# float64 weights to float32 words: the sign's word made on GpSimd, the magnitude scaled on ScalarE

## The chip, the cores and the metric

The kernel runs on one core of one Trainium2 chip. The metric is the device time of one execution in microseconds (us); the time given for a kernel is the median of its runs. PE is TensorE, DVE is VectorE, ACT is ScalarE, POOL is GpSimd, and SP is SyncE, whose queue issues most of the transfers.

## The reference, cut to what matters

Three blocks are computed in a row: windowed attention with a linear bias (4 batches, 8 heads, 576 positions, 64 columns a head), a gated MLP with a mixing over positions (width 512, inner width 1024), and a second MLP with a convolution of three taps and a sigmoid gate.

```python
x = attention(q, k, v)                       # (4, 576, 512)
h = gelu(x @ w_in);  u, v = h[..., :512], h[..., 512:]
v_s = einsum('ts,bsd->btd', w_sg, layernorm(v) * g_ln) + b_sg
x = x + (u * v_s) @ w_out
h = relu(x @ w_in2)
out = (h * sigmoid(conv3(h))) @ w_out2
```

`w_in`, `w_out`, the convolution's taps and the second MLP's two weights are drawn as float64 and are handed to the kernel as they are. [...]

## The kernel before, in words

Every large product is made in float32 accuracy out of three products of rounded operands: a matrix is split into a rounded part `hi` and a remainder `lo` (`split`, L244), and PE adds hi*hi, hi*lo and lo*hi. A weight therefore goes through a load, the conversion of its float64 words to float32 (`narrowed`, L310), a rounding (on ACT as a rule) and a remainder (on POOL as a rule) before PE can use it.

`narrowed` takes a staged block of n numbers in each of 128 partitions, as 2n 32-bit words: `low` is every first word, `high` every second one, which holds the sign, 11 bits of exponent and 20 bits of mantissa. It reads the high word as if it were a float32. The steps are: the magnitude of the high word into the tile `wa` (an Abs on ACT at L322 if `act_abs` is set, else a bit mask on DVE at L324); a clamp of it between W_LOW and W_HIGH on DVE (L328), which bounds the exponent; a mask and a shift left by three bits (L329); the sign bits of the high word are or-ed in (L330); and the low word's upper three bits, shifted down by 29, are or-ed in (L331). The last two have two tensor inputs. So DVE does four steps for a block whose magnitude comes from ACT, and five for the others.

`w_in` comes in eight pieces of 512 columns (`w_in_load` L345, `w_in_piece` L350, steps `j` and `i` of the order), the second half first; ACT makes the magnitude for the four pieces of the second half and for the first one of the first half. Four staging buffers are used in turn, so the load of the fifth piece waits until the first has been converted. `w_out` comes in eight pieces of 256 columns (`w_out_piece` L373, step `o`), all with the magnitude on DVE; their `wa` tiles have two buffers in turn. The second MLP's weights go through the same function later (`w2_piece` L382), as do the taps (L894).

The order of the work is a list of steps written by hand (L54 to L130). A framework then orders each engine's instructions out of it by priority and by a simulated timeline, except where an instruction is kept behind the one written before it on its engine (`keep_in_program_order`). Up to about 80 us the four batches' first attention heads, the pieces of w_in and the first products run interleaved; from there on the first batch's mixing (`m_sg` L827, step `G`), the weights' scaling (`a_norm` L495, step `N`, through `scaled` L233), the transposes of the attention weights (`a_transpose` L532, step `T`) and the product with w_out (`m_wo` L848, step `W`).

Where several engines could do a step, a planner picks one while the program is written out. It keeps a ledger of nanoseconds for each engine, which never falls more than SLACK (6000 ns) behind PE's:

```python
def book(eng, ns):
    load[eng] = max(load[eng], load["pe"] - SLACK) + ns
def pick(costs):
    eng = min(costs, key=lambda e: max(load[e], load["pe"] - SLACK) + costs[e])
    book(eng, costs[eng])
```

The costs are formulas of the columns n. `narrowed` books 67 + 0.52 n on DVE for the clamp (L327) and 200 + 2.6 n for the other steps (L332). Of the steps that the planner can place, those of interest here are the scaling of attention weights (DVE or POOL), the gate's rounding (ACT, DVE or POOL) and its remainder (DVE or POOL), and the copies of transposed weights out of PSUM (ACT or DVE).

Of the kernel before, what the change touches and what calls it, by code (L numbers as in the profile page):

```python
# [11 lines left out]
AF = mybir.ActivationFunctionType  # L12
ALU = mybir.AluOpType
# [5 lines left out]
HF = FF // 2  # L19
# [16 lines left out]
NVN = 4  # L36
# [12 lines left out]

W_LOW = 2.0**-15  # L50
W_HIGH = 122879.9921875


def _steps():  # L54
# [80 lines left out]
def attention_gmlp_glu_kernel(  # L135
# [21 lines left out]
    nc = tc.nc  # L157
    PSUM = bass.MemoryType.PSUM

    def f(ap):  # L160
        return ap.bitcast(F32)
# [39 lines left out]
# [6 lines that stand above are left out]
        return eng  # L207
# [36 lines left out]
    def split(hi, lo, src, kind=None, done=None):  # L244

        ins = copy(hi, src, kind is None, ON[kind + " hi"] if kind else "act dve")
        if done is not None:
            done[:] = [ins.ins.name]
        return tt(lo, src, f(hi), ALU.subtract, ON[kind + " lo"] if kind else "dve")
# [7 lines left out]
    mpool = p1.enter_context(tc.tile_pool(name="mpool", bufs=2))  # L257

    with tc.using_default_side("right"):
        pa = ExitStack()  # L260
        apool = pa.enter_context(tc.tile_pool(name="apool", bufs=2))
# [27 lines left out]
    for i in range(NP):  # L289
        st = cpool.tile([P, 18], F32, name=f"st{i}")  # L290
# [16 lines left out]

    STAGE = dict(st=S, vn=1024, w64=512)

    def narrowed(src, n, pool, tag, bufs, spool, stag, sbufs, act_abs=False):  # L310

        if spool is None:
            st = src
        else:
            st = spool.tile([P, STAGE[stag]], U32, tag=stag, name="w64", bufs=sbufs)
            dma = nc.sync.dma_start(st[:, : 2 * n], src)
            later(dma)
        words = st[:, : 2 * n].rearrange("p (n w) -> p n w", w=2)
        low, high = words[:, :, 0], words[:, :, 1]
        a = pool.tile([P, 256 if tag == "wa" else 512], U32, tag=tag, name="wa", bufs=bufs)[:, :n]  # L320
        if act_abs:
            tc.keep_in_program_order(nc.scalar.activation(f(a), f(high), AF.Abs))  # L322
        else:
            ins = tc.keep_in_program_order(nc.vector.tensor_scalar(a, high, 0x7FFFFFFF, None, op0=ALU.bitwise_and))  # L324
            if last_hi:
                tc.add_manual_dep(ins.ins, last_hi[-1], follow, reason="high part first")
        clamp = nc.gpsimd if pick({e: c for e, c in dict(dve=67 + 0.52 * n, pool=147 + 0.93 * n).items() if e in ON["clamp"]}) == "pool" else nc.vector  # L327
        tc.keep_in_program_order(clamp.tensor_scalar(f(a), f(a), W_LOW, W_HIGH, op0=ALU.max, op1=ALU.min))  # L328
        nc.vector.tensor_scalar(a, a, 0x07FFFFFF, 3, op0=ALU.bitwise_and, op1=ALU.logical_shift_left)  # L329
        nc.vector.scalar_tensor_tensor(a, high, 0xC0000000, a, op0=ALU.bitwise_and, op1=ALU.bitwise_or)  # L330
        nc.vector.scalar_tensor_tensor(a, low, 29, a, op0=ALU.logical_shift_right, op1=ALU.bitwise_or)  # L331
        book("dve", 200 + 2.6 * n)  # L332
        return f(a)

    def cols(w, k, c0, n):

        return w.bitcast(U32)[:, k, 2 * c0 : 2 * (c0 + n)]

    w64, last_in, last_win, last_hi = {}, [], [], []

    def later(dma):

        tc.add_manual_dep(dma.ins, last_in[0].ins.name, follow, reason="later")
# [4 lines left out]
        last_in[:] = [tc.keep_in_program_order(nc.sync.dma_start(st, w_in.bitcast(U32)[:, half, k, :]))]  # L348

    def w_in_piece(half, k):  # L350
        a = narrowed(w64.pop((half, k)), HF, mpool, "u", 4, None, "vn", NVN, half == 1 or k == 0)
        if half:
            split(winh[:, k, HF:], winl[:, k, HF:], a, "win")
        else:
            sl = slice(k * P, (k + 1) * P)
            last_win[:] = [split(winh[:, :, sl], winl[:, :, sl], a.rearrange("p (k n) -> p k n", k=NK), "win" if k else "win u", None if k else last_hi)]

    def staged(src, dtype):
        st = mpool.tile([P, S], dtype, tag="x", name="wst", bufs=8)[:, : src.shape[-1]]
        later(nc.sync.dma_start(st, src))  # L360
        return st
# [11 lines left out]
    def w_out_piece(k, half):  # L373
        if k == half == 0:
            kept["wo"] = w1pool.tile([P, NK, 2, 2, 256], F32R, tag="wo", name="wo")
        st = staged(cols(w_out, k, half * 256, 256), U32)
        a = narrowed(st, 256, apool, "wa", 2, None, "x", 8)
        split(kept["wo"][:, k, half, 0, :], kept["wo"][:, k, half, 1, :], a, "wo")

    p2pool = []  # L380
# [491 lines left out]
    def constants(i):  # L872
# [11 lines left out]
        B=rotations,  # L884
        k=constants, l=z_load, v=z_vload, c=z_scores, e=z_exp, n=z_norm, t=z_transpose, z=z_av, j=w_in_load, L=a_load, M=a_vload, C=a_scores, E=a_exp, N=a_norm, T=a_transpose, A=a_av,
        X=a_xsplit, V=m_v, U=m_u, G=m_sg, W=m_wo, i=w_in_piece, g=w_sg_piece, o=w_out_piece, a=w2_piece,
    )

# [230 lines left out]
```

## Time and profile before

| what | value |
|---|---|
| median of 3 runs | 543.5 us (542.86 to 543.69) |
| the profiled execution's own time | 543.29 us |
| its span, from the first to the last instruction | 541.1 us |
| mean granted clock of TensorE | 0.997 of full speed |
| busy share PE, DVE, ACT, POOL | 96%, 68%, 48%, 45% |
| instructions | 11980 |

Shares of the span are averages over stretches with different limits. A group of instructions is read as: line, engine, operation, output<-input by the program's names, shapes and count, then busy time, the mean length of one, and the idle time before them with what ended it.

### The profile page before, as it was taken

To read this page: it belongs to the slowest core of one execution; us is meant where nothing else is said; L and a number is where in the kernel's file an instruction comes from. 1 tells how busy PE (TensorE), PEld (TensorE's weight loads), DVE (VectorE), ACT (ScalarE), POOL (GpSimd) and SP (SyncE) were. 2 spreads that over 40 slices of the span, in tenths; PEclk is the share of its full clock that TensorE was granted. 3 is DMA by queue.
4 is the path that set the end of the run, shared out by engine and by line. 5 is a ranking of instruction groups with operands and counts; after the bars stand their busy time and mean duration, and the time that the engine had idled before them with its cause. 6 is when DMAs were issued, how large, how long until landed. Compare 5 with 4: busy or idle time off the path is not lost.

```text
span 541.1 us, 11980 instructions
## 1 busy us (share of the span) xinstructions
PE 520.7 (96%) x4548; PEld 474.7 (88%) x4548; DVE 367.7 (68%) x959; ACT 258.7 (48%) x673; POOL 243.2 (45%) x383
## 2 busy tenths in 40 slices
PE   8997989999998999999999999999999999999997
PEld 6776879898898988989988999998998999999887
DVE  4999798754878875879767688687567354654300
ACT  6694578342458451376534434452554333444310
POOL 2444238542146363246453344245586545465500
PEclk9999989999999999999999999999999999999999
DMA  8974541433261765243643433902202100100011
GB/s 290 394 241 175 150 121 52 148 113 98 89 201 37 218 187 190 82 124 92 173 144 115 155 101 131 337 13 52 75 21 81 66 22 19 42 21 27 33 39 59
DMA packets 33209, 63.93 MB, mean 118 GB/s; under 512 B 3968, under 2 KB 13952, under 8 KB 33152
## 3 DMA queue, kind: packets, MB, share of 16 engines
q1 hardware_dynamic: 33008, 63.04, 35.8%
q8 instruction: 36, 0.59, 0.5%
q14 instruction: 21, 0.17, 0.1%
q10 hardware_dynamic: 144, 0.13, 0.1%
HBM read 48.47 MB, written 14.68 MB: 117 GB/s over the span
## 4 chain that ended last, share of the span: by engine, by line
PE 62%; DVE 14%; ACT 9%; POOL 7%; DMA 5%; issue 3%; SPq 0%; ACTq 0%; DVEq 0%; POOLq 0%
PE psg L213 31%; PE psv L213 7%; PE pso L213 6%; PE psu L213 5%; PE o L213 4%; ACT t L186 3%; PE pss L213 3%; PE sc L213 3%; POOL t L242 3%; PE pT L515 2%; DMA w<-in_w_in_dram 2%; DVE t L451 1%; DVE wa L330 1%; DMA kq<-in_qk_dram 1%; DVE wa L328 1%
## 5 line engine op out<-in xcount | busy, mean ns | idle before, releaser
L213 PEld LDWEIGHTS psg<-x2g,w 128*128 128x128 f32 x768 | 103.1, 188 | 2.4 <-ACT hb L973 0.7
L213 PE MATMUL psg<-x2g,w 128*128 128x256 f32 (+1 forms) x768 | 104.6, 294 | 0.6 <-ACT hb L973 0.5
L213 PE MATMUL psg<-wout,gh 128*128 128x512 f32 (+1 forms) x272 | 80.1, 378 | 0.0
L186 ACT ACTIVATE t<-t,st 128x192 f32<-128x192 f32 (+1 forms) x144 | 61.9, 431 | 15.0 <-DVE st L451 15.0
L213 PE MATMUL pss<-wsg,vn 128*128 128x256 f32 (+1 forms) x448 | 63.6, 298 | 3.6 <-DVE t L843 3.0
L213 PEld LDWEIGHTS pss<-wsg,vn 128*128 128x128 f32 x448 | 60.5, 190 | 4.7 <-DVE t L843 4.0
L977 DVE SCALAR_TENSOR_TENSOR cc<-hb,cw,cc 128x576 f32<-128x576 f32 x32 | 26.6, 832 | 46.9 <-POOL cc L242 46.9
L213 PEld LDWEIGHTS psg<-wout,gh 128*128 128x128 f32 x272 | 49.8, 188 | 8.7
L213 PE MATMUL psu<-xg,win 128*128 128x320 f32 (+1 forms) x384 | 54.2, 298 | 2.6 <-ACT win L222 1.7
L213 PEld LDWEIGHTS psu<-xg,win 128*128 128x128 f32 x384 | 51.7, 188 | 3.7 <-ACT win L222 1.8
L213 PE MATMUL pso<-gh,wo 128*128 128x256 f32 (+1 forms) x256 | 51.8, 300 | 0.5 <-DVE t L843 0.5
L213 PE MATMUL psg<-wout,gl 128*128 128x512 f32 (+1 forms) x136 | 50.9, 378 | 0.0
L213 PE MATMUL psv<-win,xg 128*128 128x512 f32 x192 | 47.6, 398 | 0.9 <-DVE wa L328 0.9
L242 POOL TENSOR_SCALAR cc<-hb,cw 128x576 f32<-128x576 f32 x32 | 28.3, 885 | 42.7 <-ACT hb L973 42.7
L451 DVE CUSTOM_DVE_ANT_0 t<-sc,tab 128x192 f32<-128x192 f32 (+1 forms) x144 | 40.4, 335 | 5.4 <-PE sc L213 5.0
L973 ACT ACTIVATE hb<-psg 128x576 f32<-128x576 f32 x32 | 20.7, 651 | 47.5 <-PE psg L213 45.0
L213 PEld LDWEIGHTS psv<-win,xg 128*128 128x128 f32 x192 | 35.5, 188 | 8.7 <-ACT win L222 1.0
L231 DVE TENSOR_TENSOR gg<-cc,hb 128x576 f32<-128x576 f32 x32 | 30.1, 943 | 17.2 <-ACT cc L186 17.0
L213 PEld LDWEIGHTS pso<-gh,wo 128*128 128x128 f32 x256 | 40.3, 188 | 1.7 <-DVE t L843 1.2
L213 PE MATMUL pso<-gl,wo 128*128 128x256 f32 (+1 forms) x128 | 36.9, 301 | 1.3 <-POOL gl L231 0.6
L231 POOL TENSOR_TENSOR t<-t,u 128x256 f32<-128x256 f32 (+1 forms) x32 | 27.2, 854 | 18.6 <-DVE t L843 18.4
L231 POOL TENSOR_TENSOR gl<-gg,gh 128x512 fp32r<-128x512 f32 x24 | 33.7, 1404 | 0.6
(101 smaller groups left out, 960.4 us busy)
## 6 DMA issues: line engine op xcount, KB each, us to landing
V<-in_v_dram SPq DMA_DIRECT2D x12, 704.0 KB, 4.7
x2s<-x2d SPq DMA_DIRECT2D x16, 288.0 KB, 2.9
w<-in_w_in_dram SPq DMA_DIRECT2D x8, 512.0 KB, 7.5
w<-in_w_out_dram SPq DMA_DIRECT2D x16, 256.0 KB, 3.2
w<-in_w_in_dram SPq DMA_DIRECT2D x16, 256.0 KB, 2.8
wout<-w2d SPq DMA_DIRECT2D x8, 512.0 KB, 6.0
q<-in_q_dram SPq DMA_DIRECT2D x12, 320.0 KB, 4.0
out_dram<-ot SPq DMA_DIRECT2D x15, 256.0 KB, 2.0
```

What stands on the lines that cost most here:

```text
L186: ins = nc.scalar.activation(*args, **kw)
L213: return nc.tensor.matmul(out, lhsT, rhs, start=start, stop=stop, **kw)
L231: return (nc.vector if eng == "dve" else nc.gpsimd).tensor_tensor(dst, a, b, op=op)
L242: e.tensor_scalar(dst, src, col, 1.0, op0=ALU.mult, op1=ALU.mult)
L328: tc.keep_in_program_order(clamp.tensor_scalar(f(a), f(a), W_LOW, W_HIGH, op0=ALU.max, op1=ALU.min))
L330: nc.vector.scalar_tensor_tensor(a, high, 0xC0000000, a, op0=ALU.bitwise_and, op1=ALU.bitwise_or)
L451: nc.vector.tensor_tensor_reduce(e, bank, table, scale=-SCALE, scalar=3e38, op0=ALU.add, op1=ALU.min, accum_out=mx)
L515: ins = nc.tensor.transpose(ps[:, i * P : (i + 1) * P], src, ident)
L973: nc.scalar.activation(h[:, 1 : S + 1], ps[:, 256 : 256 + S], AF.Relu)
L977: nc.vector.scalar_tensor_tensor(cc, h[:, 0:S], cw[:, 0, c : c + 1], cc, op0=ALU.mult, op1=ALU.add)
```

## The change

For the pieces of w_in and w_out (`apart` = 1) the steps are replaced. ACT makes the magnitude and multiplies it by 2^-48 in the same step, for all sixteen pieces. POOL multiplies the high word, read as a float32, twice by 2^-140 and writes it back in place, strided: what is left is a zero with the word's sign. DVE clamps the magnitude between the bounds scaled by the same 2^-48. After that the exponent's field lies so that the shift by three needs no mask. DVE shifts the low word down by 29 and ors the signed zero in, in place in the staging buffer; then it shifts the magnitude left by three and ors that word in. DVE so does three steps for every piece. The planner is told 200 + 1.6 n on DVE in all, for the clamp and both other steps. The second MLP's weights and the taps stay as they were, and so do the loads and buffers.

```diff
@@ -49,6 +49,8 @@
 
 W_LOW = 2.0**-15
 W_HIGH = 122879.9921875
+W_DOWN = 2.0**-48
+W_GONE = 2.0**-140
 
 
 def _steps():
@@ -307,7 +309,7 @@
 
     STAGE = dict(st=S, vn=1024, w64=512)
 
-    def narrowed(src, n, pool, tag, bufs, spool, stag, sbufs, act_abs=False):
+    def narrowed(src, n, pool, tag, bufs, spool, stag, sbufs, act_abs=False, apart=0):
 
         if spool is None:
             st = src
@@ -318,6 +320,19 @@
         words = st[:, : 2 * n].rearrange("p (n w) -> p n w", w=2)
         low, high = words[:, :, 0], words[:, :, 1]
         a = pool.tile([P, 256 if tag == "wa" else 512], U32, tag=tag, name="wa", bufs=bufs)[:, :n]
+        if apart:
+            tc.keep_in_program_order(nc.scalar.activation(f(a), f(high), AF.Abs, scale=W_DOWN))
+            ins = tc.keep_in_program_order(
+                nc.gpsimd.tensor_scalar(f(high), f(high), W_GONE, W_GONE, op0=ALU.mult, op1=ALU.mult)
+            )
+            clamp = nc.gpsimd if apart == 2 else nc.vector
+            tc.keep_in_program_order(
+                clamp.tensor_scalar(f(a), f(a), W_LOW * W_DOWN, W_HIGH * W_DOWN, op0=ALU.max, op1=ALU.min)
+            )
+            nc.vector.scalar_tensor_tensor(low, low, 29, high, op0=ALU.logical_shift_right, op1=ALU.bitwise_or)
+            nc.vector.scalar_tensor_tensor(a, a, 3, low, op0=ALU.logical_shift_left, op1=ALU.bitwise_or)
+            book("dve", 200 + 1.6 * n)
+            return f(a)
         if act_abs:
             tc.keep_in_program_order(nc.scalar.activation(f(a), f(high), AF.Abs))
         else:
@@ -348,7 +363,7 @@
         last_in[:] = [tc.keep_in_program_order(nc.sync.dma_start(st, w_in.bitcast(U32)[:, half, k, :]))]
 
     def w_in_piece(half, k):
-        a = narrowed(w64.pop((half, k)), HF, mpool, "u", 4, None, "vn", NVN, half == 1 or k == 0)
+        a = narrowed(w64.pop((half, k)), HF, mpool, "u", 4, None, "vn", NVN, half == 1 or k == 0, 1)
         if half:
             split(winh[:, k, HF:], winl[:, k, HF:], a, "win")
         else:
@@ -374,7 +389,7 @@
         if k == half == 0:
             kept["wo"] = w1pool.tile([P, NK, 2, 2, 256], F32R, tag="wo", name="wo")
         st = staged(cols(w_out, k, half * 256, 256), U32)
-        a = narrowed(st, 256, apool, "wa", 2, None, "x", 8)
+        a = narrowed(st, 256, apool, "wa", 2, None, "x", 8, apart=1)
         split(kept["wo"][:, k, half, 0, :], kept["wo"][:, k, half, 1, :], a, "wo")
 
     p2pool = []
```

## Rows read from the trace of the kernel before

**Rows 1.** The page: busy us by engine (part 1), granted clock in forty slices (part 2).

```profile
PE 520.7 (96%) x4548; PEld 474.7 (88%) x4548; DVE 367.7 (68%) x959; ACT 258.7 (48%) x673; POOL 243.2 (45%) x383
...
PEclk9999989999999999999999999999999999999999
```

**Rows 2.** Stretches of the span: busy us and count (x) by engine, granted clock, DMA.

```profile
13.50:76.80 63.30, 55.92 (x663) 45.84 (x662) 57.25 (x166) 42.03 (x112) 25.68 (x33) 1.00 0.63 223
76.80:101.00 24.20, 22.85 (x210) 21.06 (x210) 22.11 (x74) 17.20 (x68) 19.74 (x35) 0.93 0.25 80
101.00:150.00 49.00, 49.00 (x537) 44.86 (x536) 31.51 (x111) 18.79 (x47) 15.03 (x33) 1.00 0.35 114
150.00:541.00 391.00, 381.76 (x2986) 353.68 (x2984) 250.46 (x570) 171.62 (x413) 179.17 (x272) 1.00 0.31 98
```

**Rows 3.** What PE waited for, 13.5 to 101 us: total, times, longest.

```profile
PE sc L213 <- DVE st L451: 2.1, 1, 2.1
PE psu L213 <- ACT win L222: 1.7, 1, 1.7
PE o L213 <- ACT ph L222: 1.2, 2, 1.0
PE psv L213 <- DVE wa L328: 0.9, 1, 0.9
```

**Rows 4.** Short stretches around PE's longest wait, columns as in rows 2.

```profile
76.00:78.00 2.00, 1.23 (x20) 1.26 (x22) 2.00 (x15) 2.00 (x10) 0.00 (x0) 0.68 0.78 296
78.00:80.00 2.00, 2.00 (x14) 1.88 (x10) 1.97 (x8) 2.00 (x10) 0.16 (x1) 0.50 0.05 9
80.00:82.00 2.00, 2.00 (x18) 2.00 (x18) 2.00 (x17) 2.00 (x11) 1.32 (x2) 0.97 0.82 230
```

**Rows 5.** VectorE's steps on wa, 13.5 to 76.8 us: ns least/median/most, first and last start.

```profile
L328 DVE TENSOR_SCALAR wa<-wa x11: 274/416/1385, 13.6 to 69.1; 128x512 f32<-128x512 f32 x8, 128x256 f32<-128x256 f32 x3
L329 DVE TENSOR_SCALAR wa<-wa x11: 267/427/1525, 14.0 to 69.7; 128x512 uint32<-128x512 uint32 x8, 128x256 uint32<-128x256 uint32 x3
L330 DVE SCALAR_TENSOR_TENSOR wa<-w,wa x8: 675/688/1655, 15.0 to 53.0; 128x512 uint32<-128x512 uint32 x8
...
L324 DVE TENSOR_SCALAR wa<-wst x4: 274/283/286, 59.0 to 74.0; 128x256 uint32<-128x256 uint32 x4
L324 DVE TENSOR_SCALAR wa<-w x3: 415/420/421, 37.1 to 50.1; 128x512 uint32<-128x512 uint32 x3
```

**Rows 6.** VectorE in order of time, near 22 us: start us, length us, instruction.

```profile
22.34 1.52 DVE L329 TENSOR_SCALAR wa<-wa 128x512 uint32<-128x512 uint32 x1
```

**Rows 7.** GpSimd in order of time, near 22 us, same columns.

```profile
22.32 1.27 POOL L231 TENSOR_TENSOR win<-wa,win 128x512 fp32r<-128x512 f32 x1 [0.88 <-ACT win L222]
```

**Rows 8.** GpSimd's groups by form, whole span: busy us, mean ns, idle before.

```profile
L242 POOL TENSOR_SCALAR t<-t,r 128x192 f32<-128x192 f32 x49 | 22.7, 476 | 0.0
...
L231 POOL TENSOR_TENSOR win<-wa,win 128x512 fp32r<-128x512 f32 x8 | 11.2, 1402 | 8.4 <-ACT win L222 7.1 <-DVE win L224 1.3
...
L225 POOL TENSOR_SCALAR wh<-wa 128x256 fp32r<-128x256 f32 x20 | 9.2, 461 | 41.6 <-DVE wa L331 41.4
...
L231 POOL TENSOR_TENSOR wo<-wa,wo 128x256 fp32r<-128x256 f32 x8 | 6.3, 793 | 11.3 <-ACT wo L222 11.3
...
L225 POOL TENSOR_SCALAR x2g<-x2s 128x576 fp32r<-128x576 f32 x4 | 3.1, 778 | 0.0
```

**Rows 9.** ScalarE's magnitude step L322.

```profile
L322 ACT ACTIVATE wa<-w x17: 424/438/686, 12.9 to 332.3; 128x256 f32<-128x256 f32 x12, 128x512 f32<-128x512 f32 x5
```

**Rows 10.** VectorE's steps on wa, 76.8 to 101 us.

```profile
L329 DVE TENSOR_SCALAR wa<-wa x5: 280/286/347, 77.8 to 95.2; 128x256 uint32<-128x256 uint32 x5
L330 DVE SCALAR_TENSOR_TENSOR wa<-wst,wa x5: 409/417/523, 78.2 to 95.5; 128x256 uint32<-128x256 uint32 x5
```

**Rows 11.** VectorE's groups by form, 76.8 to 101 us.

```profile
L242 DVE TENSOR_SCALAR t<-t,r 128x192 f32<-128x192 f32 x6 | 2.8, 513 | 0.0
...
L224 DVE COPY ph<-pT 128x512 f32<-128x512 f32 x3 | 2.0, 676 | 0.0
```

## The prediction, made before the changed kernel was run

> **What bounds the kernel now.** I read the page's totals first, then the stretches of the span, then what TensorE waited for, and only then single steps. The totals show TensorE (PE) busy for 520.7 of 541.1 us and VectorE (DVE) for 368 [rows 1]. Read alone, that says nothing done to DVE can matter. The stretches say where it can [rows 2]. From 13.5 to 76.8 us DVE is busy 57.25 of 63.3 us and PE only 55.92, so PE stands idle for 7.4 us in a stretch where DVE is nearly full. From 76.8 to 101 us DVE is busy 22.1 of 24.2 us, GpSimd (POOL) 19.7, and PE is idle for 1.4. From 101 to 150 us PE is busy throughout, and in the 391 us after that it idles for 9.2 us in all. So time can be won before 101 us, and PE's queue carries a head start won there to the end.
>
> Of PE's waits before 101 us, two end behind DVE [rows 3]: 2.1 us for the statistics of the masked scores (line 451), and 1.7 us for a piece of w_in, which ScalarE (ACT) rounds after DVE's last step on it. The other two shown, 1.2 and 0.9 us, I lay to ACT's order and don't count. The 2.1 us wait, which ends at 76.8 us, has a second price: behind it the granted clock reads 0.68, 0.50 and 0.97 in three stretches of 2 us [rows 4], the middle one being the 1.2 GHz level. That is 2 x (0.32 + 0.50 + 0.03) = 1.7 us of TensorE's speed, and the only dip in the span [rows 1].
>
> **The change part by part.** The profiled execution took 543.29 us (span 541.1 and 2.2 around it), 0.2 below the median of 543.5; I add the terms to the median. About 0.2% (1.1 us) is what a measurement of this kernel can tell from no change.
>
> *Front, 13.5 to 76.8 us: DVE.* All eight pieces of w_in fall here, with three pieces of w_out and the first step of a fourth. The masking step L329 goes everywhere: 8 x 0.43 + 3 x 0.27 = 4.2 us at undisturbed lengths [rows 5]. The absolute value L324 moves to ACT: 3 x 0.42 + 4 x 0.28 = 2.4 us [rows 5]. The clamp L328 stays, as do two two-input steps, at the length of L330, 0.69 us [rows 5]; that one of them now writes every second word in place I count at nothing, since L324 reads every second word at the price of a dense step. DVE is relieved of 6.6 us.
>
> *Front: POOL.* Added are 8 one-input steps of 512 columns and 3 to 4 of 256, on every second word, in place. No row shows such a step. Dense one-input steps take 0.46 us at 256 columns and 0.78 at 576, so 0.71 at 512; two-input ones take 0.79 and 1.40 [rows 8]. The sum is 8 x 0.71 + 4 x 0.46 = 7.5 us by the first and 14.4 by the second. I take 7.5, as the step has one input. POOL has the room (25.7 busy of 63.3), and rests more than half of the stretch. What it costs DVE is the question: DVE's L329 at 22.34 us took 1.52 us for 0.43 of work, next to a POOL step that began at 22.32 and ran 1.27 [rows 6, 7]. The longest L328, L329 and L330 here lost 0.97 + 1.10 + 0.97 = 3.0 us against their medians [rows 5]. Laid against 25.7 us of POOL work, that is 0.12 us per us, 0.9 us for the new steps. At worst each shuts DVE out for its whole length, 7.5 us. The new step starts when the clamp does, more often than chance, so I take a quarter: 1.9 us. DVE's net relief is then 4.7 us, with ends of 5.7 and -0.9.
>
> *Front: ACT* gains 3 x 0.67 + 4 x 0.44 = 3.8 us [rows 9] and is busy 42 of 63.3; its idle time covers that. Without that cover the exponentials queued behind these steps would come later, and the scores' banks with them.
>
> *What PE gets back.* I take the whole 2.1 us wait, as DVE's queue arrives there 4.7 us less burdened. Of the 1.7 us wait I take 0.9: DVE's queue is earlier, but the piece's own chain is no shorter. Before, magnitude, clamp, mask and two combining steps were 0.67 + 0.43 + 0.43 + 2 x 0.69 = 2.9 us; now they are 0.67 + 0.71 + 1.38 = 2.8, the clamp beside POOL's step, and if the two exclude each other 3.2. Of the 1.7 us of clock I take half, 0.85, as a shorter idle may be left. Sum: 3.8 us.
>
> *Second stretch, 76.8 to 101 us.* Five L329 and four L324 go, at 0.29 us each [rows 10]: DVE -2.6 us. But the planner now books 845 ns less DVE time for each w_in piece (67 + 0.52 x 512 + 200 + 2.6 x 512 before, 200 + 1.6 x 512 after) and 456 less for each w_out piece, and books neither ACT's nor POOL's new step. Worked through its own formulas, choices flip in steps N1.0 to T1.0 and nowhere later. Five scalings of attention weights (net) and three gate remainders go from POOL to DVE; two gate roundings and three copies of transposed weights, two of them 512 wide, go from ACT to DVE. On DVE that is 5 x 0.51 + 3 x 0.42 + 2 x 0.29 + 2 x 0.68 + 0.3 = 6.1 us [rows 10, 11], the gate remainder at the price of L330 and the rounding at that of L329. Net DVE +3.5 us, with 2.1 us of slack. POOL loses 5 x 0.48 + 3 x 0.79 = 4.8 us and gains 4 x 0.46 = 1.8 [rows 8]. Before, POOL's chain was the late one here, and PE lost 1.4 us; now DVE is the later. Of the 3.5 - 2.1 = 1.4 us too much I charge PE half, 0.7 us, since products with w_sg cover PE through most of the stretch and DVE enters with a lead. With the cover gone it would be 3.5.
>
> After 101 us nothing is changed but the start. Loads are no term: those of the last four w_in pieces wait for a buffer that a piece's last DVE step frees, and that step stays last and comes no later; the loads queued behind them on SP follow.
>
> Forecast: 543.5 - 3.8 + 0.7 = **540.4 us**. Its own range is 536.8 (the 2.1, 1.7 and 1.7 us in full and the 1.2 us behind ACT, nothing charged) to 542.4.
>
> **The rivals.** *The relief is eaten.* If POOL's new steps shut DVE out for their whole 7.5 us, 6.6 - 7.5 = -0.9 us is left, PE waits as before, and the time is 543.5, at worst 544.4. For it: clamp and sign step become ready together, and [rows 6, 7] show a full exclusion. Against it: at the front, 25.7 us of POOL work went by with only a small part of it lost by DVE. The Trainium skill, SBUF — State Buffer, section "Who interferes with whom", says that GpSimd and a VectorE instruction in a two-port mode block each other for the whole instruction, and that two-input VectorE steps contend with GpSimd's reads as well. Rows 6 and 7 agree with that where they meet; how often they meet, the rule doesn't say. Chance 0.19.
>
> *The planner overloads DVE.* Place: 82 to 101 us, steps N1.0 to T1.0. Price: 3.5 us on DVE, and PE's transposed weights for the first pair of the next batch then come from DVE's queue in place of ACT's. It decides once DVE brings a lead of less than 1.4 us into 76.8 us. With half of the front's gain (1.9 less about 0.3 of clock): 543.5 - 1.6 + 3.5 = 545.4 us. For it: DVE has the least slack there. Against it: POOL, whose chain was the late one, is relieved by 3.0 us. Chance 0.18.
>
> *The sign step is not a one-input step in cost*, through its strides or the tiny factor. At 1.40 us a w_in piece's chain is 0.67 + 1.40 + 1.38 = 3.45 us, 0.55 longer, and DVE's queue waits for POOL eight times. Half of these 4.4 us exposed, less 1.2 us of relief, gives 544.5. Chance 0.05.
>
> **How the numbers follow.** Forecast 0.58, all of it faster. Eaten: 0.16 same and 0.03 slower. Planner: 0.18 slower. Sign step: 0.02 same and 0.03 slower. Faster 0.58, same 0.18, slower 0.24. The range goes from the forecast's low end, 536.8, to the planner rival's 545.4.
>
> **What would show it.** Right: L329's place is empty, DVE's busy time to 76.8 us falls by about 5 us, the 2.1 us wait and the dip of the clock go or shrink, and the moved scalings, remainders and copies are seen on DVE after 82 us. Wrong: POOL's sign step over 0.8 us at 512 columns, clamps stretched to its length, VectorE waiting for POOL in front of its first combining step, or new PE waits between 88 and 101 us behind DVE's copies.

## The result, and the profile after

The changed kernel takes 548.95 us (median of 6 runs, 547.58 to 549.98) where the kernel before takes 543.3 (6 runs, 542.72 to 543.69). The ratio is 1.0102, with a 95% interval of 1.0082 to 1.0121: slower by 5.65 us, outside the range of the prediction. The profiled execution took 548.06 us, with a span of 546.2.

The page of the changed kernel, busy time by engine and granted clock, to be laid beside [rows 1]:

```profile
PE 520.7 (95%) x4548; PEld 474.8 (87%) x4548; DVE 364.1 (67%) x945; ACT 261.0 (48%) x679; POOL 247.6 (45%) x391
...
PEclk9999997999999999999999999999999999999999
```

PE is busy for as long as before, so by this page the 5.1 us that the span grew by are PE standing idle. The same stretches as in [rows 2], with the same columns:

```profile
13.50:76.80 63.30, 56.76 (x677) 46.37 (x678) 52.95 (x155) 42.60 (x112) 34.00 (x46) 1.00 0.63 227
76.80:101.00 24.20, 20.30 (x188) 19.78 (x182) 18.88 (x64) 18.43 (x70) 16.69 (x30) 0.86 0.16 49
101.00:150.00 49.00, 46.74 (x521) 42.50 (x520) 31.61 (x108) 18.45 (x46) 12.91 (x29) 1.00 0.35 118
```

DVE is relieved in the front by 57.25 - 52.95 = 4.3 us, but PE's idle time there falls only from 7.4 to 6.5 us. In the second stretch it rises from 1.35 to 3.90 us, although DVE is 3.2 us less busy, and the granted clock falls from 0.93 to 0.86. From 101 to 150 us, where PE never stood still, it now idles for 2.26 us. After 150 us it loses another 1.2. The sum, with 0.15 won before 13.5 us, is -0.15 - 0.84 + 2.55 + 2.26 + 1.24 = 5.1 us.

What PE waited for, 13.5 to 101 us (compare [rows 3]), and, as the last row, from 101 us on:

```profile
PE pss L215 <- DVE t L858: 3.9, 1, 3.9
PE psu L215 <- ACT v L188: 2.1, 2, 1.3
PE psu L215 <- POOL win L233: 2.0, 2, 1.3
...
PE o L215 <- DVE ph L226: 2.3, 1, 2.3
```

The 2.1 us wait for the statistics of the masked scores is gone. In its place stands one of 3.9 us, for the gate's step on the mixing's product (L858; L843 before), which has to read a tile `pss` out of PSUM before PE can fill it anew. The last row is the planner's: a 512-wide copy of transposed weights now on DVE. The clock around the long wait, to be read against [rows 4]:

```profile
82.00:84.00 2.00, 0.00 (x0) 0.00 (x0) 2.00 (x13) 2.00 (x10) 0.52 (x1) 0.77 0.04 14
84.00:86.00 2.00, 1.16 (x5) 1.16 (x6) 2.00 (x7) 2.00 (x11) 1.13 (x3) 0.50 0.00 0
86.00:88.00 2.00, 2.00 (x12) 2.00 (x11) 1.13 (x4) 2.00 (x11) 2.00 (x5) 0.50 0.00 0
88.00:90.00 2.00, 2.00 (x11) 2.00 (x11) 1.13 (x2) 2.00 (x11) 2.00 (x5) 0.52 0.00 0
```

TensorE stands at 1.2 GHz for two stretches and nearly the whole of a third, where before it did for one.

Why does a relieved DVE come late to L858? What DVE itself waited for, from 13.5 us up to its first L858 (84.31 us), in the changed kernel:

```profile
DVE r L703 <- POOL r L702: 2.9, 3, 1.7
DVE wa L330 <- ACT wa L324: 2.7, 1, 2.7
DVE wsg L233 <- ACT wsg L224: 2.7, 2, 1.5
DVE w L332 <- POOL w L326: 1.7, 3, 0.6
```

The third row was there before; the first was 1.0 us up to the same step (82.55 us then), the others were not there. A wait of 1.3 us for POOL's step `rs` shrank to 0.4. Most of the work taken from DVE became waiting. The 2.7 us wait for ACT's magnitude leads one engine further. ACT in order of time, the changed kernel (`ACT_TABLE_LOAD` is the step of 1.28 us that stands between the gelu and the exponentials; below it is called the table load):

```profile
73.96 0.43 ACT L324 ACTIVATE wa<-wst 128x256 f32<-128x256 f32 x1
74.30 0.43 ACT L188 ACTIVATE u<-psu 128x320 f32<-128x320 f32 x1
77.50 0.41 ACT L224 CAST wo<-wa 128x256 fp32r<-128x256 f32 x1 [2.77 <-DVE wa L333]
77.81 0.43 ACT L188 ACTIVATE u<-psu 128x320 f32<-128x320 f32 x1
78.26 1.28 ACT L188 ACT_TABLE_LOAD   x1
79.55 0.40 ACT L188 ACTIVATE t<-t,st 128x128 f32<-128x128 f32 x1
...
81.52 0.41 ACT L324 ACTIVATE wa<-wst 128x256 f32<-128x256 f32 x1
```

and in the kernel before:

```profile
73.57 0.41 ACT L222 CAST wo<-wa 128x256 fp32r<-128x256 f32 x1 [0.20 <-DVE wa L331]
73.89 0.76 ACT L186 ACTIVATE u<-psu 128x320 f32<-128x320 f32 x2
74.66 1.28 ACT L186 ACT_TABLE_LOAD   x1
75.96 0.40 ACT L186 ACTIVATE t<-t,st 128x128 f32<-128x128 f32 x1
```

Before the table load the old order rounds three pieces of w_out on ACT (at 64.55, 69.81 and 73.57 us). The new order rounds four (65.24, 69.48, 71.32 and 77.50). The fourth waits 2.77 us for DVE's last step on its piece, and the gelu, the table load and the next heads' exponentials queue behind it: they begin at 79.55 instead of 75.96 us, 3.6 us later. DVE in order of time shows why that last step is late:

```profile
74.29 0.42 DVE L332 SCALAR_TENSOR_TENSOR wst<-wst 128x256 uint32<-128x256 uint32 x1
74.63 0.90 DVE L233 TENSOR_TENSOR vn<-v,vn 128x512 fp32r<-128x512 f32 x1
75.46 0.35 DVE L466 CUSTOM_DVE_ANT_0 t<-sc,tab 128x192 f32<-128x192 f32 x1
...
77.04 0.42 DVE L333 SCALAR_TENSOR_TENSOR wa<-wa,wst 128x256 uint32<-128x256 uint32 x1
```

The scaling of vn, five masks and another piece's clamp stand between the two combining steps. The next magnitude, at 81.52 us, sits behind four of the late exponentials; DVE's clamp waits for it, with masks and L858 behind the clamp. PE's chain follows: the first transposes of the new weights start at 92.56 us and not 88.88, 3.7 us later.

PE in order of time, the changed kernel (before, the row that answers to the first began at 78.80 us):

```profile
77.35 3.60 PE L215 MATMUL pss<-wsg,vn 128*128 128x256 f32 x28
84.84 7.88 PE L215 MATMUL pss<-wsg,vn 128*128 128x256 f32 x42 [3.90 <-DVE t L858]
92.56 1.58 PE L530 MATMUL pT<-ident,t 128*128 128x128 f32 x13
```

PE did arrive 1.45 us earlier at the mixing; it then waited 3.90 us, and at the lower clock the 70 products took 3.60 + 7.88 us in place of 10.24. That gives the 3.7 us: -1.45 + 3.90 + 1.24. So PE is late at the transposes by the wait at L858 and the clock behind it, and not because the transposes themselves waited for exponentials; that both are late by nearly the same is not shown to be more than chance.

### The profile page after: what moved, and what is told of

It reads as the page before. It is cut to its first block, busy times and chain, and to the rows that moved or that the text cites. A ratio compares the mean times of both kernels' runs of the same rounds, so it can differ in the third digit from the quotient of the medians.

```text
span 546.2 us, 11996 instructions
## 1 busy us (share of the span) xinstructions
PE 520.7 (95%) x4548; PEld 474.8 (87%) x4548; DVE 364.1 (67%) x945; ACT 261.0 (48%) x679; POOL 247.6 (45%) x391
## 4 chain that ended last, share of the span: by engine, by line
PE 59%; DVE 18%; POOL 6%; ACT 6%; DMA 6%; issue 5%; SPq 1%; POOLq 0%; DVEq 0%; ACTq 0%
PE psg L215 31%; PE pso L215 6%; PE pss L215 6%; PE psv L215 4%; PE o L215 4%; PE sc L215 3%; DVE t L466 3%; PE pT L530 3%; PE psu L215 2%; ACT t L188 1%; DMA V<-in_v_dram 1%; DVE t L244 1%; POOL t L244 1%; DMA w<-in_w_in_dram 1%; DVE gg L233 1%
## 5 line engine op out<-in xcount | busy, mean ns | idle before, releaser
L215 PE MATMUL pss<-wsg,vn 128*128 128x256 f32 (+1 forms) x448 | 65.0, 303 | 8.1 <-DVE t L858 6.8
L215 PEld LDWEIGHTS pss<-wsg,vn 128*128 128x128 f32 x448 | 62.0, 195 | 9.0 <-DVE t L858 7.5
L188 ACT ACTIVATE t<-t,st 128x192 f32<-128x192 f32 (+1 forms) x144 | 61.9, 431 | 15.3 <-DVE st L466 15.2
```

Of the source, the lines that this page charges most:

```text
L188: ins = nc.scalar.activation(*args, **kw)
L215: return nc.tensor.matmul(out, lhsT, rhs, start=start, stop=stop, **kw)
```

## The experiments

In each set the kernel before ran again beside the experiments, and each ratio, with its 95% interval, is against those runs. The medians of the kernel before were 543.61 us in the first set, 542.94 in the second, 543.28, 543.65 and 544.11 in the others, so times of different sets are comparable to about 1 us.

**First set: halves of the change.** e1 plans the change as before:

```diff
-            book("dve", 200 + 1.6 * n)
+            book("dve", 67 + 0.52 * n)
+            book("dve", 200 + 2.6 * n)
```

> The whole change, but the planner is told the same VectorE time for a piece as before (67 + 0.52 n and 200 + 2.6 n). Theory A (the loss is w_out's magnitude on ScalarE: it stands in ScalarE's queue behind a table load and exponentials, VectorE's clamp waits for it, and line 858 behind the clamp holds PSUM banks for TensorE): the waits of about 2.7 us on VectorE and 3.9 us on TensorE stay, and the time stays 3 to 6 us above before, 546.5 to 549.5. Theory B (the planner's moves of 13 choices to VectorE cost the time): the 2.3 us wait of the product with v for VectorE's copy goes, and the time falls to 542 to 544.5. Theory C (GpSimd's sign step shuts VectorE out in the front): unchanged against the change, 547 to 549.

Measured: 548.66 us, ratio 1.0085 [1.0055, 1.0115]. The wait for the copy goes (2.26 to 0.25 us), the 3.9 us wait stays, and the time stays, as theories A and C had it. The bookings aren't what costs, or not alone.

e2 leaves w_out as before, e3 w_in:

```diff
 # e2
-        a = narrowed(st, 256, apool, "wa", 2, None, "x", 8, apart=1)
+        a = narrowed(st, 256, apool, "wa", 2, None, "x", 8)
 # e3
-        a = narrowed(w64.pop((half, k)), HF, mpool, "u", 4, None, "vn", NVN, half == 1 or k == 0, 1)
+        a = narrowed(w64.pop((half, k)), HF, mpool, "u", 4, None, "vn", NVN, half == 1 or k == 0)
```

> The change for w_in alone; w_out's pieces go the way of before. Theory A: the two waits of 2.7 and 3.9 us are gone, what is left is the front's gain or nothing, 541.5 to 544. Theory B: most of the planner's moves stay, as w_in has 6.8 of the 10.4 us of changed bookings: 546 to 549. Theory C: the front's part stays, all eight pieces of 512 columns being in it: 546 to 549.

> The change for w_out alone; w_in's pieces go the way of before. Theory A: the waits of VectorE for ScalarE's magnitude and of TensorE for line 858 are there, 545.5 to 549. Theory B: 3.6 of 10.4 us of changed bookings are left, 543 to 546. Theory C: only the 256-column sign steps are left, 543 to 545.

Measured: e2 548.74 us, 1.0089 [1.0054, 1.0123], with a 2.9 us wait at L858; e3 547.67 us, 1.0056 [1.0034, 1.0077], with 4.1 us. Theory A fails at e2, where w_out's magnitude is not on ACT. Either half brings more than half of the loss (0.89% and 0.56% against 1.02%), so the halves don't add, and no price per piece explains it. e2 also shows that a late table load needs no fourth rounding of w_out: three stand ahead of it there, as before, and what is late is a rounding of vn (72.75 us before) that waits for DVE:

```profile
75.46 0.62 ACT L224 CAST vn<-v 128x512 fp32r<-128x512 f32 x1 [1.16 <-DVE v L801]
```

Its exponentials start at 78.05 us.

e4 does the work of before under the change's bookings:

```diff
-        book("dve", 200 + 2.6 * n)
+        book("dve", 200 + (1.6 if apart else 2.6) * n)
```

(the clamp's own booking is left out too).

> The kernel before with the planner told the smaller VectorE time for w_in's and w_out's pieces, and nothing else changed: the planner's moves alone. Theory A: 542.5 to 545. Theory B: 546 to 549, with TensorE's product with v waiting for VectorE's copies between 95 and 106 us. Theory C: 542.5 to 545.

Measured: 550.27 us, 1.0110 [1.0078, 1.0142], more than any theory had. In its profile the clock had dipped to 0.83 between 40 and 60 us, ahead of the first instruction whose order differs, so it was run again as e18, below.

**Second set: one wait at a time.** e5 makes w_out's magnitude on DVE again (the clamp then scales and bounds from below); e6 moves the sum ahead of the reciprocal (L702) from POOL to DVE; e7 leaves POOL's step out and masks the sign on DVE; e8 issues ACT's and POOL's steps of w_out one piece ahead.

Of e5 and e8 the main lines alone are shown:

```diff
 # e5, w_out
...
-                tc.keep_in_program_order(nc.scalar.activation(f(a), f(high), AF.Abs, scale=W_DOWN))
+                tc.keep_in_program_order(nc.vector.tensor_scalar(a, high, 0x7FFFFFFF, None, op0=ALU.bitwise_and))
 # e6
-        nc.gpsimd.tensor_scalar(r, stats[m][1][:, a : a + n], 1e-9, 1.0, op0=ALU.add, op1=ALU.mult)
+        nc.vector.tensor_scalar_add(r, stats[m][1][:, a : a + n], 1e-9)
 # e7
-            ins = tc.keep_in_program_order(
-                nc.gpsimd.tensor_scalar(f(high), f(high), W_GONE, W_GONE, op0=ALU.mult, op1=ALU.mult)
-            )
-            nc.vector.scalar_tensor_tensor(low, low, 29, high, op0=ALU.logical_shift_right, op1=ALU.bitwise_or)
-            nc.vector.scalar_tensor_tensor(a, a, 3, low, op0=ALU.logical_shift_left, op1=ALU.bitwise_or)
+            nc.vector.tensor_scalar(a, a, 0x1FFFFFFF, 3, op0=ALU.bitwise_and, op1=ALU.logical_shift_left)
+            nc.vector.scalar_tensor_tensor(a, high, 0x80000000, a, op0=ALU.bitwise_and, op1=ALU.bitwise_or)
+            nc.vector.scalar_tensor_tensor(a, low, 29, a, op0=ALU.logical_shift_right, op1=ALU.bitwise_or)
 # e8; apart_first holds ACT's and POOL's step
...
+        for p in range(i + (i > 0), min(i + 2, 8)):
+            st = staged(cols(w_out, p // 2, p % 2 * 256, 256), U32)
+            a = apool.tile([P, 256], U32, tag=("wa", "wh")[p % 2], name="wa", bufs=2)
+            apart_first(a, st.rearrange("p (n w) -> p n w", w=2)[:, :, 1])
+            ready[p] = st, a
...
```

> The change, but the magnitude of w_out's pieces is made on VectorE (a bit mask), and the scaling by 2^-48 rides on the clamp, whose upper bound is left out; GpSimd's sign step stays. VectorE does four steps for those pieces and waits for ScalarE at none. Theory D (the relief of VectorE up to its first line 858, 5.2 us, is lost in new waits of VectorE, 7.0 us more idle, of which 2.7 us is the wait for ScalarE's magnitude behind the table load and the exponentials): that wait goes, VectorE reaches its first line 858 at 82 to 83 us against 84.3, TensorE's 3.9 us wait shrinks to 1 to 2, and the time falls by 2 to 4 us to 545 to 547. Theory B (planner's moves): unchanged, 548 to 549.5. Theory E (the time at line 858 is set by VectorE's number of steps in front of it, not by what it waits for): with eight steps more, 0 to 2 us slower than the change, 549 to 551.

> The change, but the step that adds 1e-9 to the sums of the first batch's weights (line 702, eight times) is made on VectorE in place of GpSimd. Theory D: VectorE's waits for GpSimd in front of the reciprocal (2.9 us up to line 858) go for 8 x 0.2 = 1.6 us of work, so up to 1.3 us is won, 547 to 548.7; the 3.9 us wait of TensorE stays. Theory E: eight steps more, 549 to 550.5.

> The scaled magnitude on ScalarE for all sixteen pieces, but no step on GpSimd: VectorE masks the sign out of the high word itself, four steps a piece (clamp, shift, two combining). Theory D: the 1.7 us of waits for the sign step go, the wait for ScalarE in w_out stays; VectorE has 16 steps more (some 6 us), so line 858 is reached at 84 to 86 us and the time is 547 to 550. Theory C (GpSimd's sign step, by shutting VectorE out and standing in GpSimd's queue, is the loss): 543 to 545.

> The change, but ScalarE's magnitude and GpSimd's sign step of each w_out piece are issued one piece earlier (into four buffers in turn in place of two), so that they stand in ScalarE's queue ahead of the table load and the exponentials. Same work on each engine. Theory D: VectorE's 2.7 us wait for ScalarE is gone, line 858 is reached near 82 us, TensorE's 3.9 us wait shrinks to about 1.5, and the time is 544.5 to 546.5. Theory B: unchanged, 548 to 549.5. Theory C: unchanged or slower.

Measured: e5 546.59 us, 1.0056 [1.0028, 1.0083]. PE's longest wait up to 101 us in e5:

```profile
PE pss L215 <- DVE t L860: 4.0, 1, 4.0
```

DVE in order of time, up to its first L860 (the step that is L858 in the change):

```profile
78.78 0.43 DVE L334 SCALAR_TENSOR_TENSOR wst<-wst 128x256 uint32<-128x256 uint32 x1 [0.31 <-POOL wst L329]
...
82.97 0.17 DVE L515 TENSOR_SCALAR r<-st 128x9 f32<-128x9 f32 x1 [0.54 <-ACT t L188]
...
84.02 0.86 DVE L860 SCALAR_TENSOR_TENSOR t<-pss,gln,bsg 128x256 f32<-128x256 f32 x2
```

The wait for the magnitude is gone and PE's wait is not. From 74.75 to 84.02 us DVE has no longer wait than these two; it works, the fourth step on w_out included, and comes to the step as late as in the change (84.31). So the wait for ACT's magnitude is not by itself what makes L858 late. What orders it late in e5 isn't traced further; the exponentials are late here too (78.99 us). The time fell into the range that theory D gave, 2.4 us under the change, but not by the way that it gave: the first transposes start at 92.74 us. e6 became worse, 550.36 us, 1.0121 [1.0084, 1.0159], against theory D: its exponentials start at 82.79 us. e8 took 545.63 us, 1.0027 [0.9995, 1.0060], the best of those with POOL's step, and not told apart from the kernel before by that interval. The range was theory D's, the way again not: ACT's early magnitude waits 2.9 us for its load, the exponentials start at 80.83 us, and the step that is L858 in the change comes at 85.85.

e7 took 546.98 us, 1.0057 [1.0038, 1.0076], between the two ranges expected. Its exponentials start at 75.98 us, as before, its longest wait at L856 (the same step) is 1.6 us, the clock doesn't dip, and the transposes start at 89.06. The front's loss is gone. What is left to see is a PE wait of 2.6 us for the planner's copies at 102 us.

**Third set: with the bookings of before.** e9 is e7 and e10 is e8, each with e1's edit. e11 is e10 with e3's edit, so that only w_out is changed.

> The kernel without GpSimd's sign step (all sixteen magnitudes on ScalarE, four VectorE steps, no step on GpSimd), with the planner told what it was told before. In e7_no_gpsimd_step, which has the change's bookings, TensorE reached line 858 no later than in the kernel before and then lost 2.56 us at 102 us to two 512-wide copies of transposed weights that the planner had moved to VectorE. If the planner's moves are what was left there: that wait is gone (below 0.5 us) and the time is 543.0 to 545.0, about 2.5 under e7's 546.98. If what is left is a loss that any new order of the second phase brings (after 110 us), the wait goes but the time stays within 545.5 to 547.5.

> The change with w_out's ScalarE and GpSimd steps one piece ahead (as in e8_wout_one_ahead, 545.63) and the planner told what it was told before. If hand-offs and bookings are separate losses that add: 543.0 to 544.8, with no PE wait over 0.6 us behind VectorE's copies at 100 to 108 us. If GpSimd's step itself is the greater part and the bookings do nothing (as e1_old_bookings, 548.66 against 548.95, suggests): 545.0 to 546.5.

> Only w_out's pieces are converted in the new way, one piece ahead, with the planner told what it was told before; w_in's pieces stay as in the kernel before. Up to about 68 us almost nothing differs from before. If GpSimd's step costs mainly by late hand-offs: 541.5 to 543.5, no slower than before, VectorE's wait for ScalarE's magnitude below 0.5 us. If GpSimd's step costs by itself, wherever it stands (locks, GpSimd's queue), or if any new order costs 1.5 to 2 us after 110 us: 544.5 to 546.5.

Measured: e9 543.6 us, 0.9990 [0.9967, 1.0014], level with the kernel before, as expected if the planner's moves are what was left; by the medians they were worth 3.4 us in e7. ACT in e9:

```profile
74.15 0.77 ACT L324 ACTIVATE wa<-wst 128x256 f32<-128x256 f32 x2
74.82 0.74 ACT L188 ACTIVATE u<-psu 128x320 f32<-128x320 f32 x2
75.58 1.28 ACT L188 ACT_TABLE_LOAD   x1
76.87 0.40 ACT L188 ACTIVATE t<-t,st 128x128 f32<-128x128 f32 x1
```

Magnitudes of w_out on ACT do no harm where nothing late stands ahead of the table load. e10 took 547.14 us, 1.0059 [1.0036, 1.0083], not below e8 and above both ranges, so bookings and hand-offs don't add up; its exponentials start at 80.99 us. e11 took 546.49 us, 1.0041 [1.0016, 1.0065], at the end of its second range, exponentials at 79.15.

**Fourth set: what of POOL's step costs.** In e12 to e14 the signs are left out. e12 has no POOL step and DVE's three steps, e13 is e12 with the bookings of before, e14 keeps POOL's step but lets nobody read it.

```diff
-            nc.vector.scalar_tensor_tensor(low, low, 29, high, op0=ALU.logical_shift_right, op1=ALU.bitwise_or)
+            nc.vector.scalar_tensor_tensor(low, low, 29, high, op0=ALU.logical_shift_right, op1=ALU.bitwise_and)
```

(for e14 the second tensor is `low` too; e12 and e13 leave out the POOL step as e7 does). e15 is the kernel before with this edit:

```diff
-        a = narrowed(w64.pop((half, k)), HF, mpool, "u", 4, None, "vn", NVN, half == 1 or k == 0)
+        a = narrowed(w64.pop((half, k)), HF, mpool, "u", 4, None, "vn", NVN, True)
```

> The change without GpSimd's step: the signs of w_in and w_out are left out (the first combining step masks the low word with the high one in place of or-ing the sign in; same length), so VectorE has its three steps and waits for ScalarE and the loads alone. Bookings as in the change. If GpSimd's step is the greater part of the loss: TensorE's wait at line 858 falls below 2 us and the time is 543 to 545.5, the rest being the planner's copies at 102 us. If ScalarE's late magnitudes are: the 3.9 us wait stays and the time is 547 to 549.

> As e12_no_sign_at_all (signs left out, no step on GpSimd, three VectorE steps), with the planner told what it was told before. This is the bound of what three VectorE steps could give if the sign came for nothing. If the relief of VectorE is worth what I predicted: 540 to 541.5. If VectorE's relief has nothing to give once its queue waits for other engines: 543 to 544.5, as e9.

> The change with GpSimd's step in place, but VectorE's first combining step reads the low word twice and not GpSimd's result, so nobody on VectorE waits for it (the signs are left out). Bookings as in the change. If the hand-off is what costs: as e12, within 0.7 us of it. If the step's own time on GpSimd and its port costs: 1.5 us or more above e12, towards 548, with VectorE waiting for GpSimd's sum ahead of the reciprocals (3 us or more in all) as in the change.

> The kernel before with one edit: the magnitudes of the last three w_in pieces are made on ScalarE, as those of the first five are. VectorE is relieved of 3 x 0.42 = 1.3 us up to 68 us. If relief of VectorE ahead of 76 us reaches TensorE's 2.1 us wait: 541.5 to 542.8. If not, because these magnitudes then come late from ScalarE's queue or because the order shifts: 543 to 544.5.

Measured: e12 547.99 us, 1.0069 [1.0039, 1.0099]; e13 546.45, 1.0049 [1.0025, 1.0074]; e14 549.82, 1.0100 [1.0057, 1.0143]. e12 came out in the range of late magnitudes without their wait: its longest PE wait is 2.5 us, for the masked scores. e13 missed both ranges. e14 lies 1.8 us above e12, as expected if the step's own time costs, but the two intervals overlap. With nothing to wait for but its load, the first combining step was ordered early and blocked DVE there. DVE's waits up to 90 us in e12:

```profile
DVE w L329 <- DMA w<-in_w_in_dram: 3.7, 2, 2.0
```

e15 took 543.65 us, 0.9989 [0.9964, 1.0014]: DVE is 57.25 - 54.41 = 2.8 us less busy in the front, the 2.1 us wait stays as it was, and nothing is won.

**Fifth set.** e16 is e13 with the first combining step kept behind the clamp, e17 is e16 with POOL's step present and unread, as in e14; e18 is e4 again.

```diff
-            nc.vector.scalar_tensor_tensor(low, low, 29, high, op0=ALU.logical_shift_right, op1=ALU.bitwise_and)
+            tc.keep_in_program_order(nc.vector.scalar_tensor_tensor(low, low, 29, high, op0=ALU.logical_shift_right, op1=ALU.bitwise_and))
```

> As e13_no_sign_old_bookings (signs left out, no GpSimd step, three VectorE steps, planner told as before), with the first combining step kept behind the clamp in VectorE's order, as in the change. If relief of VectorE is worth what I predicted once no step waits for a late producer: 540.5 to 542.5. If VectorE's relief has nothing to give in the front: 543 to 544.5, as e9 and e15.

> As e16_no_sign_kept_old_bookings, with GpSimd's sixteen steps in place, in the order of the change, but nobody waits for what they write. Against it stand e16 without the steps and e1 (548.66) with the steps awaited. If the hand-off costs most: within 1 us of e16, and 4 us or more under e1. If GpSimd's own time and port cost most: within 1.5 us of e1, 547 or more.

> The same kernel as e4_bookings_only: the work of before, planned with the change's bookings. If the bookings by themselves cost what e4 showed: 549 to 551, with TensorE's wait of 2 us or more for VectorE's copies at 100 to 108 us. If the clock's dips in e4's profile were chance and the bookings cost that one wait: 545.5 to 547.5.

Measured: e16 547.33 us, 1.0047 [1.0023, 1.0072], above both ranges. This is the idea with its sign for nothing, and it is slower than the kernel before. ACT in e16:

```profile
72.62 0.39 ACT L224 CAST wo<-wa 128x256 fp32r<-128x256 f32 x1
72.91 0.43 ACT L188 ACTIVATE u<-psu 128x320 f32<-128x320 f32 x1
76.76 0.40 ACT L224 CAST wo<-wa 128x256 fp32r<-128x256 f32 x1 [3.41 <-DVE wa L330]
...
77.84 1.28 ACT L188 ACT_TABLE_LOAD   x1
79.14 0.40 ACT L188 ACTIVATE t<-t,st 128x128 f32<-128x128 f32 x1
```

It is the picture of the change without POOL: five roundings of w_out ahead of the table load where the change has four and the kernel before three, 3.4 us of waiting, late exponentials, and a PE wait of 3.2 us at L856. From e9 it differs mainly by one DVE step less on each piece, and e9 is level with the kernel before: here less work on DVE went with a longer time. e17 took 550.65 us, 1.0107 [1.0061, 1.0153], 3.3 us above e16: that is POOL's step in place with nobody waiting for it. So its presence costs, and the hand-off to DVE isn't needed for the loss (e1, where it is awaited, took 548.66). Whether it costs by its time on POOL or by the order that the framework makes with it is not told apart: the exponentials start at 83.05 us in e17, at 79.14 in e16.

e18 took 549.5 us (10 runs), 1.0086 [1.0060, 1.0112], as expected if the bookings cost by themselves: e4 was no chance. Its exponentials are early (75.36 us) and the first transposes are where they were (88.92). PE in e18:

```profile
93.88 2.04 PE L213 MATMUL o<-ph,V 128*64 128x64 f32 x52
...
103.05 3.58 PE L213 MATMUL o<-ph,V 128*64 128x64 f32 x52 [2.53 <-DVE ph L224]
```

The second group of 52 products waits 2.53 us for DVE's copies and then runs 1.54 us longer than the first. With its start it is 2.0 us behind the kernel before (101.01 us), with its end 3.6. The rest of the 5.4 us comes later and isn't traced to a single wait. Part of it is the clock in this execution: PE worked some 9.7 us at 1.2 GHz, against 3.4 in the profile of the kernel before. Half of what is more lies before 83 us, where the order is still that of before, so the bookings can't have brought it.

**All runs together.** Start of the exponentials behind the table load, against the bookings (medians in us):

| exponentials start | bookings of before | bookings of the change |
|---|---|---|
| 75.4 to 76.9 us | before 543.3, e9 543.6, e15 543.65 | e7 546.98, e18 549.5 |
| 77.7 to 83.1 us | e1 548.66, e10 547.14, e11 546.49, e13 546.45, e16 547.33, e17 550.65 | change 548.95, e2 548.74, e3 547.67, e5 546.59, e6 550.36, e8 545.63, e12 547.99, e14 549.82 |

In the upper row the first transposes start at 88.80 to 89.06 us, in the lower at 90.06 to 95.38. (e4 is left out, for the clock's dip ahead of all this. e13 and e14 have one too, 0.74 and 0.58 of full clock from 13.5 to 20 us, and start some 2 and 3 us later for it, an estimate; they would stay in their row without it.) Each of the two, late exponentials and the new bookings, goes with a loss by itself. Together they don't add up; that PE's second group of products waits for whichever is later would explain it, and is argued. What stands late ahead of the table load differs: in the change, e1, e5 and e16 it is a rounding of w_out, in e2 one of vn, in e8 and e10 a magnitude that waits for its load.

Most of a loss is there by PE's third group of 52 products with v. It starts at 115.11 us before, at 115.61 in e9, 116.39 in e7, 117.27 in e16, 118.02 in e1, 118.67 in e18 and 118.85 in the change: 3.7 of the change's 5.1 us.

A loss also has to be read at equal clock. The kernel before takes 542.92 us at a mean granted clock of 0.997 (45 runs, medians here), 544.17 at 0.994 (23) and 546.83 at 0.987 (15). The change takes 547.66 at 0.997 and 547.58 to 549.86 at 0.994; e18 took 547.43 at 1.000, e16 545.96 and e7 545.93 to 547.01, where the kernel before has 542.88. Their losses are not the clock's. Those of e3, e11 and e13 are in large part: e3 and e13 have 546.97 to 548.00 at 0.987, e11 a median of 545.84 at 0.991, where the kernel before has 545.16 and 545.25. How much of a lower clock the new order brings about is not shown.

What is shown and what isn't: that the bookings alone cost is shown by e18 against the kernel before and by e7 against e9. That late exponentials cost is read from the traces and from the table; no run moved only the fourth rounding behind them, so that cause is argued. Inside the lower row the time doesn't follow the start closely (e8 has 80.83 us and 545.63), so something else has a share of some 2 us there. None of the versions beats the kernel before.

## Why the prediction was wrong

**DVE's relief: right.** I forecast 4.7 us less busy time in the front; it was 4.3. The terms were partly off: POOL's sign step took 0.88 us at the median for 512 columns (0.66 to 1.09), not 0.71, and a first combining step took up to 1.75 us beside POOL's work, against 0.67 at the least (ns least/median/most, first and last start):

```profile
L326 POOL TENSOR_SCALAR w<-w x8: 657/882/1094, 13.4 to 52.0; 128x512 f32<-128x512 f32 x8
L332 DVE SCALAR_TENSOR_TENSOR w<-w x8: 674/771/1751, 14.8 to 53.1; 128x512 uint32<-128x512 uint32 x8
```

**The step that failed** is the one that covers ACT's 3.8 us: "its idle time covers that". ACT's busy time hardly rose (42.03 to 42.60), and the new steps had room; in e9 all of them are on ACT and the time is that of before. What was not covered is the place of other work in ACT's queue. The sentence behind it named the danger, exponentials that come later, and gave it no price. In the new order a fourth rounding of w_out stood ahead of the table load and waited there 2.77 us. The exponentials came 3.6 us late, the next magnitude behind four of them, DVE's clamp waited 2.73 us for that, and L858 behind the clamp came 1.8 us later than before: PE waited 3.9 us. That the shorter chains on DVE are why the order changed is argued, not shown; that it changed is in the rows. e5 has shown that the wait for the magnitude can go without L858 coming earlier, so which link of this chain decides stays open.

**"I take the whole 2.1 us wait": right, and worth little.** The wait went and PE came to the mixing 1.45 us earlier. I took that as a head start to be kept. The next thing on PE's path, L858, came 1.8 us later (84.31 against 82.55 us), and the wait moved there and grew to 3.9. e15 shows the other side: 2.8 us of relief on DVE without the new order gave nothing either, as the 2.1 us wait remained.

**"Of the 1.7 us wait I take 0.9": wrong.** The wait for w_in became 2.0 us, now behind POOL, and the same products waited 2.1 us more for ACT's step on v (L188). The 0.9 us wait, which I laid to ACT's order though its row names DVE's clamp, did go. PE's idle time in the front fell by 0.84 us in all, not by 3.0.

**"Of the clock I take half": wrong in sign.** The clock of the second stretch fell from 0.93 to 0.86. As PE had no product from 82 to 84 us, what this costs is estimated from PE's busy time in the short stretches: 1.16 x 0.50 + 2 x 0.50 + 2 x 0.48 = 2.5 us, in place of the 1.7 of before.

**"I charge PE half, 0.7 us": the planner, mis-sized.** The flips came as worked out: laid beside e1, DVE has five scalings, three gate remainders, two gate roundings and three copies more between 76 and 107 us, and PE waits for the copies. But the place is 102 to 105 us, behind the stretch that I summed, and the lead that was to pay for it was not there. Alone the bookings cost 5.4 us by the medians (e18; 4.7 by the ratio), in e7 3.4, and in the change, where everything is late already, next to nothing (e1).

**The rivals.** *The planner overloads DVE* has the right engine and sign, and the new bookings are shown to suffice by themselves; at 545.4 us it was too cheap by 3.5, and in the change it adds next to nothing. *The relief is eaten* foresaw POOL and DVE in each other's way, and e17 against e16 (3.3 us) gives the presence of POOL's step a size; but e16 is slow without any such step, so this is not what decides. The Trainium skill, SBUF — State Buffer, section "Who interferes with whom", says that a VectorE step with two inputs in SBUF contends with a GpSimd step that reads SBUF. The steps of up to 1.75 us agree with that. *The sign step* was dearer by 0.17 us, and DVE waited for it 1.7 us in all, which is not what decides either.

## What to carry to other kernels

Relief of an in-order engine counts only if the steps behind the removed ones are ready: ask what each engine's queue runs into next, and for a step moved to another engine look at what stands behind it there, not at that engine's idle share. Where a planner or scheduler orders the program, run the new bookings with the old work, and the new work with the old bookings, before laying a loss to the instructions: here the bookings alone cost nearly as much as the whole change. Compare times at equal granted clock before laying a small loss to an order. A wait that goes from PE is won only if the next producer on PE's path is earlier too.

## What the runs showed of the hardware that was not expected

A granted clock of 0.5 can follow a wait of some 2 us or not. In the kernel before it followed one of 2.1 us [rows 4]. In e18 the products behind a 2.53 us wait took 3.58 us in place of 2.04; in e7 those behind 2.56 us took 2.04, and in the changed kernel the same products behind 2.26 us:

```profile
104.76 2.04 PE L215 MATMUL o<-ph,V 128*64 128x64 f32 x52 [2.26 <-DVE ph L226]
```

Executions of one program differ by several us, and the clock goes with part of it. The twelve runs of e16 go from 545.75 to 549.71 us with mean granted clocks between 1.000 and 0.987, and the median of the mean clocks is 0.996 for the kernel before (119 runs) and 0.994 for the change. By the estimate above, 2.5 - 1.7 = 0.8 of the change's loss is TensorE's speed behind its new wait. PE's busy time, 520.7 us in both profiles, doesn't show it, so the split is not shown; either way nearly the whole loss is waiting.
